# Recurrent attention and a cosine feed-forward on one core: attention matmuls in 64x64 quadrants, half of the cumulative sums, and a new order of steps

## The chip, the cores and the metric

The kernel runs on one core of a Trainium2 chip. A core has a matrix engine (PE, with its weight loads shown as PEld), a vector engine (DVE), a scalar engine that evaluates functions from tables (ACT), a general engine (POOL), a sync engine that here only issues transfers (SP), and 16 DMA engines between HBM and the on-chip memory SBUF. Matmul results land in PSUM, which has eight banks of 128 partitions by 2 KB. The metric is the device time of one execution in microseconds (us); three executions of the kernel before took 195.17, 196.28 and 196.61 us, so the median is 196.28 us.

## The reference, cut to what matters

```python
f = 1.0 / (1.0 + np.exp(-f_logit))                 # (B, H, S, D) = (4, 8, 768, 48)
for t in range(S):
    state = f[:, :, t, :, None] * state + einsum('bhd,bhe->bhde', k[:, :, t], v[:, :, t])
    y[:, :, t] = einsum('bhd,bhde->bhe', q[:, :, t], state)
x = y.transpose(0, 2, 1, 3).reshape(B * S, H * D)  # 3072 tokens x 384
h = x @ w_in                                       # 384 -> 2048
out = (h * np.cos(h)) @ w_out                      # 2048 -> 384
```

Every head holds a 48x48 state that decays row by row with a gate f and takes in one outer product per token. The output of the attention goes token by token through a feed-forward with the activation h*cos(h).

## The kernel before, in words

The recurrence is done in chunks. 256 tokens of one batch make a *pair* of chunks (12 pairs, n = 0..11, three to a batch); partition p holds the tokens 2p (even) and 2p+1 (odd), and the partitions 0..63 and 64..127 are the two chunks g = 0 and 1. For each pair these steps run, named by a prefix and the pair's number; a suffix u = 0, 1 is a half of four heads:

- `f`, `k`, `q`, `v` load the inputs (384 KB each; pairs 0 and 1, the HALVES, load f, k and q in two halves). `ex` and `ln` (lines 321, 324) make sp = ln(1 + exp(-f_logit)), which is -ln f.
- `cum` (lines 335 to 341) forms on PE the running sums of sp for every even and every odd token, and the sum of each chunk: three wide matmuls and four of two columns for each half. `eb` and `ei` (lines 350, 354) take exp of minus and plus the sums.
- `qm`, `km` (line 363) multiply q by the decay and k by its inverse and write bf16. They are transposed, on PE (`tq`, `tk`, then the copy `qkt`) or, for the pairs 4 to 11 (TURN_QK), by a transposing DMA on SP.
- `sc` (line 411) forms the scores, `am` (line 415) masks them on DVE. `ps` (line 434) forms each chunk's outer products, `st` (line 449) adds them to the state, `sz` (line 456) decays it. The state lies in a tile of 128 x (4, 2, 48) in which half of the columns stay zero, and each `sz` is two instructions on 64 partitions, r = 0, 1.
- `y` (line 473) multiplies the masked scores by v, 64 rows and 128 columns of weights at a time; `yi` (line 483) adds q times the state, with 128 rows at a time. Both add into the same two PSUM banks.
- `yb` copies the result, `tx` (line 505) transposes it on PE, `xe` copies it into x.

The feed-forward runs in *units*: units 0 and 1 are 128 tokens each (pair 0), units 2 to 12 are 256 tokens each (pairs 1 to 11). `h` (line 531) is a half of 1024 columns of the first matmul, `co` (line 536) takes the cosine on ACT as a sine, `g` (line 513) multiplies on DVE, `o` (line 547) is a quarter of the second matmul for 128 tokens, `ot` copies, `out` stores. The weights come in eight loads `w` of 768 KB, and `wc` casts them.

The order of all of this is written out by hand: ORDER lists each step with its engine (T is PE, S ACT, V DVE, G POOL, Y SP) and its buffer, and each engine works off its own steps in the order of the list; an engine that waits holds up everything that stands behind it on that engine. `zf` are 24 matmuls on zeros that only keep PE busy. Where ACT goes over from exp/ln to the sine or back, a table load stands between (lines 536 and 586).

Of the kernel before, what the change touches and what calls it, by code (L numbers as in the profile page):

```python
# [9 lines left out]
F32 = mybir.dt.float32  # L10
BF16 = mybir.dt.bfloat16
AF = mybir.ActivationFunctionType
HALF_PI = math.pi / 2.0
# [7 lines left out]
HD = H * D  # L21
NQ = DF // 512
# [12 lines left out]
zf0:T0 zsz.2:V zsp.2:V zqk.2:V zsp.0:V f0.1:S0 zf19:T1 zf21:T0 zf4:T4 zf18:T5 zf15:T4 zf11:T5  # L35
f1.0:S1 f0.0:S zqk.0:V zf8:T4 ex0.1:S ex1.0:S f1.1:Y zf17:T5 k0.1:Y0 ln1.0:S2 cum1.0:T2 eb1.0:S0
ln0.1:S0 cum0.1:T3 ex1.1:S k0.0:Y ex0.0:S ln0.0:S q1.0:Y0 qm1.0:G2 ln1.1:S ei0.1:S0 v0:Y0 tq1.0:T6
km0.1:V0 eb0.1:S1 k1.0:Y1 ei1.0:S1 km1.0:V zf14:T7 zf10:T1 cum0.0:T7 ei0.0:S km0.0:V tk1.0:T
cum1.1:T0 eb1.1:S qkt1.0:V0 q0.1:Y1 qm0.1:G eb0.0:S tk0.1:T1 f2:Y2 tq0.1:T qkt0.1:V1 q0.0:Y ex2:S
ln2:S0 q1.1:Y vb0:G0 ps0.1:T4,5 sc1.0:T2 am1.0:V0 ps0.0:T sc0.1:T6 am0.1:V1 tk0.0:T1 k1.1:Y qm0.0:G  # L40
tq0.0:T cum2.1:T2 sz0.00:V2 qm1.1:G ei1.1:S cum2.0:T qkt0.0:S2 sz0.01:V km1.1:G w0.0:Y0 wc0.0:G
zf6:T6 tq1.1:T7 tk1.1:T qkt1.1:S3 sc0.0:T0 sc1.1:T6 ei2:S2 eb2:S2 st0.1:V0 am0.0:V2 yi0.1:T4 zf12:T5
am1.1:V3 zf16:T0 sz0.10:V2 zsz.3:G v1:Y1 vb1:G1 sz0.11:V y0.0:T5 y0.1:T y1.1:T1,0 yb0.0:S0
ps1.0:T2,3 ps1.1:T y1.0:T yb0.1:V1 tx0.1:T6 w0.1:Y1 zf7:T7 yi1.0:T w0.2:Y2 tx0.0:T7 xe0.1:S0
st1.0:V1 h1.00:T4 sz1.00:V3 yb1.0:S2 zf20:T2 xe0.0:S sz1.01:V yi1.1:T w0.3:Y3 zf1:T1 w1.3:Y4 wc0.1:V
wc0.2:V k2:Y2 yb1.1:S3 zf2:T2 st1.1:V0 sz1.11:V2 wc0.3:V h1.01:T co1.0:S0 q2:Y2 zf13:T2 h0.10:T6
tx1.1:T1 wc1.3:G xe1.1:S1 sz1.10:G g1.0:V0 zqk.1:V km2.1:G0 qm2.1:G h0.01:T2 tx1.0:T0 h0.00:T
xe1.0:S qm2.0:G co0.0:S1 km2.0:G g0.0:V1 h0.11:T co0.1:S2 g0.1:V h1.10:T0 w1.2:Y2 h1.11:T co1.1:S3
h2.31:T4 h2.30:T co2.3:S0 h2.10:T2 h2.11:T h2.21:T6 g1.1:V tq2.1:T0 w1.1:Y3 wc1.1:G g2.3:V4 h2.20:T
co2.1:S1 tq2.0:T1 v2:Y2 g2.1:V wc1.2:V f3:Y0 o3.3:T4 tk2.1:T o1.3:T5 h2.01:T2 h2.00:T co2.2:S2  # L50
tk2.0:T g2.2:V co2.0:S3 qkt2.0:V4 w1.0:Y2 vb2:G2 wc1.0:G o1.2:T qkt2.1:S1 v3:Y0 g2.0:V o0.1:T6
o0.2:T ps2.1:T7 ps2.0:T sc2.0:T0 sc2.1:T2 st2.0:V1 o3.2:T o0.3:T ex3:S o1.1:T k3:Y0 am2.1:V2
am2.0:V1 sz2.01:V3 q3:Y1 f4:Y1 ln3:S2 yi2.0:T7 cum3.1:T2 sz2.00:G cum3.0:T o3.1:T ei3:S0 y2.1:T0
y2.0:T eb3:S1 f5:Y2 o0.0:T km3.1:V2 v4:Y1 km3.0:G qm3.1:G zf22:T1 q5:Y0 yb2.0:V1 vb3:S0 v5:Y2
tx2.0:T7 xe2.0:S2 yi2.1:T ps3.0:T1,2 ps3.1:T q4:Y2 qm3.0:V yb2.1:S0 sz3.00:V2 sz3.01:V tk3.0:T3
tq3.0:T qkt3.0:V2 ot0:S0 tk3.1:T7 out0:Y ex4:S tx2.1:T0 xe2.1:V o1.0:T ln4:S0 tq3.1:T ex5:S h3.11:T0
q6:Y1 ln5:S2 st3.1:V0 qkt3.1:V0 ot1:V1 o3.0:T ot3:V2 sz3.11:V3 sc3.1:T2 sc3.0:T6 k4:Y1 am3.1:V3
h3.10:T co3.1:S0 h3.30:T4 h3.31:T out1:Y am3.0:V0 co3.3:S1 g3.1:V3 h3.20:T2 f6:Y0 y3.0:T6,7 y3.1:T
yb3.0:S3 v6:Y0 yi3.1:T h3.21:T yb3.1:S2 k5:Y2 co3.2:S2 sz3.10:V h3.00:T0 tx3.1:T6 xe3.1:S3 h3.01:T
g3.3:V co3.0:S3 tx3.0:T7 xe3.0:V vb4:G1 g3.2:V cum4.1:T4 cum4.0:T ei4:S1 eb4:S0 h4.31:T6 h4.30:T  # L60
g3.0:V km4.1:G1 km4.0:G qm4.1:G h4.11:T2 h4.10:T o4.3:T0 co4.1:S0 h4.00:T4 g4.1:V2 co4.3:S1 g4.3:V
k6:Y0 o2.3:T1 h4.01:T co4.0:S2 o2.1:T qm4.0:G o4.0:T vb6:V2 o4.2:T vb5:V0 g4.0:V o4.1:T o2.2:T
cum5.1:T2 ot4:S3 cum5.0:T o2.0:T o5.3:T0 ei5:S2 tq4.1:Y3 o5.2:T eb5:S2 sc4.1:T6 ps4.1:T4,5 tq4.0:Y1
sc4.0:T2 ps4.0:T ot2:V0 km5.1:G0 qm5.1:G qm5.0:G am4.1:V2 o5.1:T st4.0:V1 km5.0:G ex6:S ln6:S0
o5.0:T ot5:V1 h4.20:T6 h4.21:T am4.0:V1 sz4.00:G2 f11:Y1 co4.2:S3 g4.2:V f8:Y2 out4:Y tq5.1:Y4
o7.3:T4 cum6.0:T0 yi4.0:T2 sz4.01:G cum6.1:T eb6:S1 o7.1:T y4.1:T3 y4.0:T o7.2:T ei6:S0 yb4.0:V1
yi4.1:T o7.0:T o6.3:T2 yb4.1:S0 st4.1:V0 sz4.10:G3 tx4.1:T5 tq5.0:Y0 ot7:S3 ex8:S sc5.0:T6 ps5.0:T3
ps5.1:T sc5.1:T0 qm6.0:V2 o6.2:T am5.0:V0 f7:Y0 tx4.0:T4 out5:Y am5.1:V3 k7:Y1 ex7:S o6.1:T km6.0:V
sz4.11:G ln7:S2 o6.0:T q8:Y2 xe4.1:S0 km6.1:V xe4.0:S h5.31:T6 h5.30:T h5.11:T0 st5.0:V1 sz5.01:G2
sz5.00:V h5.10:T h5.20:T4 h5.21:T co5.3:S0 g5.3:V1 co5.1:S1 g5.1:V yi5.0:T3 q7:Y0 h5.00:T6 co5.2:S2  # L70
g5.2:V h5.01:T co5.0:S3 k9:Y2 yi5.1:T0 y5.0:T y5.1:T yb5.1:S2 g5.0:V o8.1:T1 yb5.0:S3 o8.3:T
tx5.1:T0 tx5.0:T3 xe5.0:V1 tq6.0:Y2 xe5.1:V out3:Y qm6.1:G tq6.1:Y1 ot6:S1 ln8:S0 ps6.1:T4,5 ps6.0:T
sc6.0:T6 sc6.1:T2 am6.0:V2 sz6.01:V3 o9.0:T0 o9.2:T zsp.1:G h6.10:T6 v7:Y1 h6.11:T am6.1:V1 h6.21:T2
co6.1:S0 sz6.00:V st6.1:V0 sz6.10:G2 h6.20:T co6.2:S1 g6.1:V0 o9.1:T cum7.1:T4 cum7.0:T y6.1:T6,7
out2:Y y6.0:T f10:Y0 ex10:S g6.2:V vb7:V1 o8.2:T eb7:S0 yb6.0:S0 yi6.1:T qm7.0:G1 o9.3:T ei7:S1
o8.0:T h6.00:T2 ot9:V2 tx6.0:T0 yb6.1:V1 sz6.11:G tx6.1:T6 h6.01:T xe6.0:V2 out7:Y ot8:V0 k10:Y0
co6.0:S2 h6.30:T4 h6.31:T xe6.1:V h7.11:T0 g6.0:V h7.20:T6 co6.3:S3 h7.10:T co7.1:S0 h7.21:T km7.0:G
g6.3:V h7.01:T2 co7.2:S1 v8:Y0 vb8:V0 g7.1:V4 f9:Y2 h7.00:T co7.0:S2 km7.1:G h7.31:T4 h7.30:T
co7.3:S3 o10.0:T0 o10.2:T qm7.1:G g7.2:V o10.3:T g7.0:V v9:Y2 tq7.0:Y3 o10.1:T ex9:S sc7.0:T6
ps7.1:T1,2 tq7.1:Y0 out8:Y vb9:G2 ln9:S1 g7.3:V k8:Y1 ps7.0:T sc7.1:T4 o13.3:T3 o13.2:T ln10:S2  # L80
am7.0:V0 cum8.1:T6 cum8.0:T am7.1:V3 y7.1:T4,5 y7.0:T st7.0:V1 ei8:S2 sz7.01:V3 sz7.00:G st7.1:V0
km8.1:V0 o12.0:T1 eb8:S2 qm8.0:V yi7.0:T yb7.0:V2 qm8.1:V yi7.1:T yb7.1:S3 o13.1:T cum9.0:T6
# [575 lines left out]
```

## Time and profile before

| what | value |
|---|---|
| median of three executions | 196.28 us (195.17 to 196.61) |
| span of the profiled execution, first to last instruction | 193.8 us |
| PE busy, share of the span | 179.9 us, 93% |
| DVE busy | 143.4 us, 74% |
| ACT busy (of it 20 table loads of 1.283 us) | 137.3 us, 71% |
| POOL busy | 57.4 us, 30% |
| mean granted PE clock | 0.991 |
| moved by DMA | 34.46 MB, mean 178 GB/s |

The profiled execution's own time is shown as its span, 193.8 us; the median of the executions that were only timed is 2.5 us longer. In a row of groups the first number is the summed busy time and the second the mean duration of one in ns. Matmuls are pipelined, so the duration of one (some 200 to 330 ns) is not what it costs in a stream; that is read from the distance between starts.

### The profile page before, as it was taken

What the parts mean: (1) busy time and instruction counts of PE and PEld (TensorE: products, weight loads), DVE (VectorE), ACT (ScalarE), POOL (GpSimd) and SP (SyncE); (2) the same over time, 40 slices, a digit from 0 to 9 for tenths busy, and PEclk for the clock granted to TensorE, in tenths of its full rate; (3) what the DMA queues carried; (4) which work ended last, traced back from release to release, by engine and by line L of the source; (5) the groups of instructions that cost most, each with busy time, mean ns of one, the idle gap of its engine ahead of it and who ended that gap; (6) DMA issues with size and microseconds to landing.
All of it is one profiled execution on the core that took longest, in us unless ns stands there. A gap on an engine that the chain in (4) does not pass through costs nothing.

```text
span 193.8 us, 5919 instructions
## 1 busy us (share of the span) xinstructions
PE 179.9 (93%) x2560; PEld 132.1 (68%) x2560; DVE 143.4 (74%) x194; ACT 137.3 (71%) x168; POOL 57.4 (30%) x75
## 2 busy tenths in 40 slices
PE   7377979998899999999979999999999999999995
PEld 2255658865678767677758867776776776777762
DVE  5069999994898278579965998589598789868420
ACT  3668668686799988988599896897575494446231
POOL 2249119405410727221017302724510540100000
PEclk9879999999999999999999999999999999999999
DMA  6999999779999899998990850499990024301213
GB/s 145 261 265 346 382 314 309 182 214 263 251 285 282 191 195 174 257 257 160 317 224 5 170 144 3 95 201 189 229 231 3 3 54 98 122 3 41 85 41 122
DMA packets 74106, 34.46 MB, mean 178 GB/s; under 512 B 67424, under 2 KB 72544, under 8 KB 74080
## 3 DMA queue, kind: packets, MB, share of 16 engines
q1 hardware_dynamic: 72496, 33.50, 72.6%
q10 hardware_dynamic: 1584, 0.59, 1.3%
q8 instruction: 20, 0.33, 0.7%
q14 instruction: 6, 0.05, 0.1%
HBM read 25.17 MB, written 4.72 MB: 154 GB/s over the span
## 4 chain that ended last, share of the span: by engine, by line
PE 72%; DVE 11%; ACT 8%; issue 4%; DMA 3%; POOL 1%; ACTq 0%; DVEq 0%; POOLq 0%
PE ps L547 29%; PE ps L531 27%; DVE w_in_bf L190 3%; PE ps L473 3%; DVE am L415 3%; DMA f<-in_f_logit_dram 3%; PE ps L411 2%; PE ps L483 2%; PE ps L335 2%; PE ps L505 2%; ACT f L321 2%; ACT sp L324 1%; DVE st L449 1%; PE ps L434 1%; DVE sz L456 1%
## 5 line engine op out<-in xcount | busy, mean ns | idle before, releaser
L513 DVE TENSOR_TENSOR g<-ps,co 128x1024 bf16<-128x1024 f32 x48 | 61.4, 1307 | 19.2 <-ACT co L536 19.1
L547 PE MATMUL ps<-w_out_bf,g 128*128 128x384 bf16 x384 | 71.4, 326 | 0.0
L531 PE MATMUL ps<-x,w_in_bf 128*128 128x256 bf16 (+1 forms) x624 | 69.3, 264 | 1.5 <-DVE w_in_bf L190 1.4
L536 ACT ACTIVATE co<-ps,halfpi 128x1024 bf16<-128x1024 f32 x48 | 52.5, 1114 | 21.1 <-PE ps L531 20.5
L531 PEld LDWEIGHTS <-w_in_bf 128*128 128x128 bf16 x624 | 56.4, 98 | 11.3 <-DVE w_in_bf L190 2.4
L547 PEld LDWEIGHTS <-g 128*128 128x128 bf16 x384 | 35.0, 98 | 19.7 <-issue 0.2
L415 DVE TENSOR_TENSOR am<-ps,pmask 128x1024 bf16<-128x1024 f32 x24 | 28.6, 1218 | 3.0 <-PE ps L411 2.8
L456 POOL TENSOR_TENSOR sz<-st,b 64x192 bf16<-64x192 f32 x20 | 11.1, 555 | 50.9 <-DVE st L449 49.7
L363 POOL TENSOR_TENSOR qk<-q,b 128x384 bf16<-128x384 f32 x18 | 18.2, 1021 | 15.3 <-DMA q<-in_q_dram 8.7
L363 POOL TENSOR_TENSOR qk<-k,bi 128x384 bf16<-128x384 f32 x15 | 15.4, 1033 | 18.6 <-ACT bi L354 13.3
L536 ACT ACT_TABLE_LOAD x10 | 12.8, 1283 | 4.4 <-PE ps L531 2.0
L363 DVE TENSOR_TENSOR qk<-k,bi 128x384 bf16<-128x384 f32 x9 | 8.1, 912 | 9.4 <-ACT bi L350 6.8
L586 ACT ACT_TABLE_LOAD x10 | 12.8, 1283 | 2.6 <-issue 2.4
L190 ACT COPY x<-ps 128x384 bf16<-128x384 bf16 x13 | 6.0, 478 | 9.2 <-PE ps L505 9.2
L321 ACT ACTIVATE f<-f 128x768 f32<-128x768 f32 (+1 forms) x14 | 10.3, 748 | 2.0 <-DMA f<-in_f_logit_dram 1.9
L335 PE MATMUL ps<-sp,incl 128*128 128x384 bf16 x24 | 8.2, 340 | 3.3 <-ACT sp L324 3.1
L354 ACT ACTIVATE bi<-ps 128x768 f32<-128x768 f32 x10 | 8.1, 812 | 3.7 <-PE ps L341 1.9
L257 PE MATMUL ps<-zero 128*128 128x512 bf16 x24 | 9.3, 493 | 1.4 <-DVE zero L196 1.2
L324 ACT ACTIVATE sp<-f 128x768 bf16<-128x768 f32 (+1 forms) x14 | 10.3, 749 | 0.3
L449 DVE TENSOR_TENSOR st<-ps,sz 128x384 f32<-128x384 f32 x16 | 8.9, 554 | 2.2 <-POOL sz L456 1.4
L411 PE MATMUL ps<-qkt 48*64 48x128 bf16 x384 | 9.2, 220 | 1.0 <-ACT qkt L190 0.8
L473 PE MATMUL ps<-vb,am 64*128 64x48 bf16 x384 | 7.4, 180 | 1.9 <-DVE g L513 1.1
(61 smaller groups left out, 174.9 us busy)
## 6 DMA issues: line engine op xcount, KB each, us to landing
v<-in_v_dram SPq DMA_DIRECT2D x12, 384.0 KB, 5.8
out_dram<-ot SPq DMA_DIRECT2D x24, 192.0 KB, 2.2
f<-in_f_logit_dram SPq DMA_DIRECT2D x10, 384.0 KB, 5.2
k<-in_k_dram SPq DMA_DIRECT2D x10, 384.0 KB, 5.9
q<-in_q_dram SPq DMA_DIRECT2D x10, 384.0 KB, 5.8
g<-in_moe_w_in_dram SPq DMA_DIRECT2D x4, 768.0 KB, 9.7
g<-in_moe_w_out_dram SPq DMA_DIRECT2D x4, 768.0 KB, 5.8
k<-in_k_dram SPq DMA_DIRECT2D x4, 192.0 KB, 5.0
```

The lines of the kernel that those rows point to most:

```text
L321: nc.scalar.activation(out=flat(t.ap), in_=flat(t.ap), func=AF.Exp, scale=-1.0)
L324: nc.scalar.activation(out=s.ap[:, :, :, 0:D], in_=swap(t.ap), func=AF.Ln, bias=1.0)
L363: G.step(f"{nm}{n}.{u}", ("POOL", "DVE"), lambda e, u=u, j=j, src=src, dec=dec: eng(e).tensor_mul(out=qkp[u][j].ap[:, :, :, 0:D], in0=swap ...
L411: nc.tensor.matmul(o[t, r, 2 * a + x, :].rearrange("p (e n) -> p e n", e=2), lhsT=qkv(u)[s, 1, a, g, x, :], rhs=qkv(u)[s, 0, a, g, :, :], ...
L415: G.step(f"am{n}.{u}", ("DVE",), lambda e, u=u, sc=sc: nc.vector.tensor_mul(out=am[u].ap.rearrange("p r b n -> p (r b n)").rearrange("p (y ...
L456: eng(e).tensor_mul(out=new.ap[s, :, r, :].rearrange("p (u a) n -> p u a n", u=2), in0=ap()[s, :, r, :].rearrange("p (u a) n -> p u a n", ...
L473: nc.tensor.matmul(py[g].ap[:, D * i:D * i + D], lhsT=am[u].ap[t, h % 2, h // 2 * 2 + x, :], rhs=vb.ap[t, i, x, :], start=(py[g].first and ...
L513: nc.vector.tensor_mul(out=o.rearrange("p b (n e) -> p b e n", e=2), in0=ph.ap.rearrange("p (b e n) -> p b e n", e=2, n=64), in1=co.ap.rea ...
L531: nc.tensor.matmul(ph.ap[:, i * T:(i + 1) * T].rearrange("p (g t) -> p g t", t=C), lhsT=w_in_bf[:, kk, f0:f0 + 128], rhs=xa[:, :, kk, :], ...
L536: G.step(f"co{m}.{j}", ("ACT",), lambda e, ph=ph, co=co: nc.scalar.activation(out=co.ap, in_=ph.ap, func=AF.Sin, bias=halfpi), reads=[ph], ...
L547: nc.tensor.matmul(po.ap[:, 0:DM], lhsT=gT.ap[:, j, i * C:(i + 1) * C], rhs=w_out_bf[:, j, :], start=(po.first and j == 4 * s), stop=(po.f ...
L586: nc.scalar.preload_act_table_set("natural_log_exp_and_others")
```

## The change

Six things are changed at once.

1. **Cumulative sums.** `cum` forms the sums at odd tokens only: one PSUM bank for a whole pair, two matmuls of 384 columns and eight of two columns (for the cut pairs 0 and 1, two of 192 and four small ones for each half). The sums at an even token differ from those at the odd token behind it by one gate, so q at even tokens is multiplied by 1/f of the odd token and k by f of the odd token. New steps do this: `fx` (ACT, exp(-sp) of the odd tokens), `qa` (DVE, (exp(-f_logit) + 1) * q) and `ka` (POOL or DVE, f * k). `eb` and `ei` are half as wide, and `qm`, `km` read the same factor for even and odd tokens.
2. **Compact states.** The state is a tile of 128 x (4, 48) without zeros; `st` is half as wide, `sz` is one instruction on 128 partitions in place of two on 64, and its buffers need no zeroing.
3. **`y` in quadrants.** Each matmul of `y` is cut into two of 64 output partitions: 768 in place of 384.
4. **`yi` in quadrants.** With the compact state `yi` works on 64 rows and 64 columns: 320 matmuls in place of 136. Each of its two steps writes both banks, one row half for each.
5. **One layout of `qkt`** for both ways of transposing.
6. **A new ORDER** for all steps, with new engines and buffers for many of them.

```diff
+        def lead_q(e, t, w):
+            eng(e).scalar_tensor_tensor(out=w.ap[:, :, 0, :], in0=t.ap[:, :, 1, :], scalar=1.0, in1=w.ap[:, :, 0, :],
+                                        op0=ALU.add, op1=ALU.mult)
+
+        def gate_of(e, t, s):
+            nc.scalar.activation(out=t.ap[:, :, 0, :], in_=s.ap[:, 1, :, 0:D], func=AF.Exp, scale=-1.0)
+
+        def lead_k(e, t, w):
+            eng(e).tensor_mul(out=w.ap[:, :, 0, :], in0=w.ap[:, :, 0, :], in1=t.ap[:, :, 0, :])
...
-            nc.tensor.matmul(o4, lhsT=incl, rhs=w[:, 0:1, :, 0:D].broadcast_to([128, 2, 4, D]),
-                             start=True, stop=False)
-            nc.tensor.matmul(o4[:, 0], lhsT=strict, rhs=w[:, 1, :, 0:D], start=False, stop=False)
-            nc.tensor.matmul(o4[:, 1], lhsT=incl, rhs=w[:, 1, :, 0:D], start=False, stop=False)
...
+            for x in range(2):
+                nc.tensor.matmul(o[:, :, 0:HB], lhsT=incl,
+                                 rhs=w[:, x, :, 0:D].rearrange("p (u h) d -> p u h d", u=un),
+                                 start=(x == 0), stop=False)
...
-            for r in range(2):
-                def decay(e, g=g, r=r, new=new, ap=ap):
-                    s = slice(64 * r, 64 * r + 64)
...
+            def decay(e, g=g, new=new, ap=ap):
+                tot = bt.ap[:, :, HB:].rearrange("p u (a g) -> p u a g", g=2)[:, :, :, g]
...
-                    for g in range(2):
-                        t = slice(64 * g, 64 * g + 64)
-                        i = 4 * u + h
-                        nc.tensor.matmul(py[g].ap[:, D * i:D * i + D], lhsT=am[u].ap[t, h % 2, h // 2 * 2 + x, :],
...
+                    for z in range(2):
+                        for g in (1, 0):
+                            t, w, i = slice(64 * g, 64 * g + 64), slice(64 * z, 64 * z + 64), 4 * u + h
+                            nc.tensor.matmul(py[g].ap[w, D * i:D * i + D],
+                                             lhsT=am[u].ap[t, h % 2, h // 2 * 2 + x, w],
...
+            for a in range(4):
+                for z in range(2):
+                    for r in range(2):
+                        g, h = (r + swap_g) % 2, 2 * a + r
...
+                        nc.tensor.matmul(py[g].ap[w, D * h:D * h + D], lhsT=qkv(a // 2)[t, 0, a % 2, g, z, :],
+                                         rhs=before[g].ap[t, a, :], start=(py[g].first and a == 0),
+                                         stop=(py[g].final and a == 3))
```

How the instructions stand after it: 10 matmuls in a pair's `cum` in place of 14 (12 for the cut pairs), but 568 more in `y` and `yi`; 10 table loads in place of 20; nine input loads issued from ACT's queue in place of three; all four casts of w_in on POOL (before: three on DVE); 14 `fx`, 14 `qa` and 14 `ka` (11 on POOL, 3 on DVE); `sz` 9 on DVE and 11 on POOL (before 20 and 20). The order of PE spends all 24 zero matmuls ahead of the first scores (before: 11 of them), does the sums of the pairs 2 and 3 and all attention of the pairs 0 and 1 but the transposes `tx1` before the first `h`, and then takes the attention of two pairs together, several steps in a row, where the order before spread them singly between `h` and `o`. The first steps of each engine after the change: PE ... sc1.0 tx0.1 tx0.0 cum3 cum2 y1.1 yi1.0 y1.0 h1.01; DVE am0.1 qa1.0 qkt1.1 sz0.0 qm1.0 st0.1 am0.0 st1.0 qkt1.0 am1.1 yb0.1 xe0.1 am1.0 st1.1 xe0.0 yb1.0 xe1.0 xe1.1 qa2 qm2.0 qm2.1 g1.0; POOL km0.1 ka0.0 ka1.1 km0.0 qm0.0 qm1.1 zero ka1.0 km1.0 sz0.1 sz1.0 and the four casts of w_in.

## The prediction

> **What bounds the kernel now.** I read the page first, then the stretches of 10 us, then PE in order of time, then the chain of work that ended last. PE is busy 93% of the span and holds 72% of the chain:
>
> ```profile
> span 193.8 us, 5919 instructions
> ...
> PE 179.9 (93%) x2560; PEld 132.1 (68%) x2560; DVE 143.4 (74%) x194; ACT 137.3 (71%) x168; POOL 57.4 (30%) x75
> ...
> PE 72%; DVE 11%; ACT 8%; issue 4%; DMA 3%; POOL 1%; ACTq 0%; DVEq 0%; POOLq 0%
> ```
>
> The chain says where PE starts to run without gaps. Ahead of this stretch stand DVE's states and its casts of w_in:
>
> ```profile
> 23.94 3.41 DVE w_in_bf L190 x2
> 27.35 0.47 DVE st L449
> 28.02 0.29 issue
> 28.31 1.77 DVE w_in_bf L190
> 30.12 5.46 PE ps L531 x66
> ```
>
> So there are two parts: a head of 30.1 us that other engines set, and PE in a nearly closed stream to its last `o` at 190.3. In the stream a step costs the distance from its start to the next start, not its duration:
>
> ```profile
> 114.09 0.42 PE L411 MATMUL ps<-qkt 48*64 48x128 bf16 x16
> 114.34 0.42 PE L434 MATMUL ps<-vb,qk 64*64 64x48 bf16 x32
> 114.59 0.42 PE L411 MATMUL ps<-qkt 48*64 48x128 bf16 x16
> 114.95 1.47 PE L547 MATMUL ps<-w_out_bf,g 128*128 128x384 bf16 x8
> 116.26 0.33 PE L335 MATMUL ps<-sp,incl 128*128 128x384 bf16 x1
> 116.42 0.25 PE L337 MATMUL ps<-sp,strict 128*128 128x192 bf16 x1
> ...
> 116.59 0.24 PE L341 MATMUL ps<-half,sp 128*128 128x2 bf16 x4
> 116.69 0.32 PE L335 MATMUL ps<-sp,incl 128*128 128x384 bf16 x1
> ...
> 117.19 0.58 PE L473 MATMUL ps<-vb,am 64*128 64x48 bf16 x32
> 117.70 0.82 PE L547 MATMUL ps<-w_out_bf,g 128*128 128x384 bf16 x4
> 118.45 0.53 PE L483 MATMUL ps<-sz,qkt 128*64 128x96 bf16 x16
> 118.92 0.82 PE L547 MATMUL ps<-w_out_bf,g 128*128 128x384 bf16 x4
> ```
>
> Prices from such distances: `h` 0.655 us (0.67 in units 0 and 1), `o` 0.65, `sc` 0.235, `ps` 0.13 for 16 matmuls in quadrants (two steps from 114.34 to 114.59), `cum` 0.43 for a half (116.26 to 116.69). `sc` ahead of `o` takes 0.36 in place of 0.25: when the form of the tiles changes, some 0.095 us are added. Less that, `y` costs 0.21 and `yi` 0.18 (0.17 in the pairs 0 to 3); `tx` 0.167, a transposing step 0.222. From 30.12 to 190.32 these prices sum to 154.9, so PE idles only 5.3 us in 160.2. From the last `o` to the end are 3.5 us.
>
> **The change, PE's work.** In `cum`, 116.26 to 116.42 gives 0.16 for a wide matmul and 116.59 to 116.69 gives 0.027 for a small one: a pair costs 2 x 0.16 + 8 x 0.027 = 0.54, was 0.86: -3.8 over 12 pairs. `y` becomes 32 matmuls in quadrants, a form that `ps` has with the same 48 columns: two times 0.125 = 0.25, was 0.21: +1.0 over 24 steps. Its bounds: 0.20 if the four quadrants pass at twice the rate of the two row tiles in `y` now (-0.2), 0.41 if they pass no faster than those (+4.8); I take `ps`, the same shape. `yi`: before, 14 steps at 0.18 and 6 at 0.17, 3.5; after, 16 of 16 matmuls at 0.125 and 8 of eight at 0.08, 2.6: -0.9. Changes of form in PE's order fall from 69 to 46: -2.2. Together -5.9.
>
> The Trainium skill speaks against cutting `y`: "TensorEngine Tiling (Array Packing)", Instruction Overhead, gives a small matmul a floor of some 60 cycles and warns against splitting a dimension that is already small. By that page, at the page's clock of 2.4 GHz, four quadrants would take 32 x 25 / 4 ns = 0.20 a step, an estimate, and the sum would be 1.2 us lower; the row of `ps` has 0.25, and the sum goes by it.
>
> From the first `h` on, the new order holds: `h` 63.0, `o` 62.4, `cum` of pairs 4 to 11 4.3, transposes 1.8, `sc` 4.7, `ps` 2.4, `y` 5.0, `yi` 2.2, `tx` 3.7, 38 changes of form 3.6: **153.1 us**, with no zero matmul in it.
>
> **The head.** The new order wants all attention of pairs 0 and 1 (but `tx1`) before `h1.01`. Followed by hand: the first gates land at 4.6 as now (both halves of f0 are the first issue of their queues, at 0.73). ACT does `ex` and `ln` at 0.55 each; with half-wide `eb`, `ei`, `fx` (0.3 to 0.5 for 192 columns, between nothing and the 0.49 for 384) it is free at 11.7 and copies `qkt0.1` (1.0); `sc0.1`, then `am0.1` at 13.3. From there DVE is the chain: `am` 4 x 1.2, `qkt` 2 x 0.68, two `st` and one `sz` at 0.35 (192 columns, row of `sz`), `qa1.0` 0.35, `qm1.0` 0.56, `yb` 0.55, `xe` 0.35: 9.0, and 13 gaps of 0.03: 22.7. `y1.0` and `yi1.0` follow; `h1.01` starts at **23.4**. What must not be later: POOL's row of steps from `km0.1` at 8.6 to the first cast of w_in ends at 18 to 19; the landings, one half load each 0.75 us as now and 2.0 for 768 KB, bring w0.1 at 20.2 behind f3 and f2, cast at 21.7. That is 1.7 us of cover; w0.2 and w0.3, cast at 27.0 and 29.0, are wanted at 29.6 and 31. The eleven zeros ahead of `cum1.0` cost 2.4 us at full clock, 4.7 at the half clock of now's first ones (0.43 apart); at 7.4 they end by 9.8 or 12.1, while `ln1.0` is done at 9.9, so up to 2.2 are uncovered.
>
> **The stream.** After 23.4 PE keeps lockstep with `g` through units 0 to 2 (1.31 for two `h`, 1.31 for `g`); `g1.0` starts at 28.3 behind `qa2` and two `qm2`, and o0.0 waits 0.9. Further waits by the same hand count: `sc2.0` for `qkt2.0` on ACT 0.8, `h4.11` for `xe3.0` behind a table load 0.75, smaller ones 0.6: 3.1 until `h6.20` at 83. For the rest I take what the order before loses from 83 on, 3 us, since DVE has 73 us of work there beside PE's 97. Idle together **6.0**.
>
> DVE's new operations are `qa` (128 x 384 from two SBUF operands; the nearest row is L363 on DVE). That row shows a cost of its own:
>
> ```profile
> 10.99 0.56 DVE L363 TENSOR_TENSOR qk<-k,bi 128x384 bf16<-128x384 f32 x1 [6.58 <-ACT bi L350]
> 11.76 2.30 DVE L363 TENSOR_TENSOR qk<-k,bi 128x384 bf16<-128x384 f32 x2 [0.21 <-ACT bi L350]
> ```
>
> Alone it takes 0.56, two beside POOL's multiplies took 1.2 each, and once (154.68) 2.52; the 15 of them average 0.79, an excess of 0.24. On the path lie some 8 in the head and 13 between `h1.01` and `h6.20`, where PE has 56.6 us of steps and DVE 53.5: 21 x 0.24 = 5.0, half of it on the path, **2.5**; bounds 0 and 5. The Trainium skill, "SBUF — State Buffer", section Who interferes with whom, calls this an exclusive lock: a DVE operation with two SBUF inputs waits out a POOL operation that reads SBUF. The 2.52 agrees with it, the eleven of 0.56 or less, seven of them beside POOL work, show that it does not always strike; rival 2 is this mechanism.
>
> Off the path: ACT loses 10 table loads (12.8), 6.5 to 9 of `eb` and `ei`, gains 6.3 of `fx`, 4.2 of `vb` and six issues at 0.5: ACT never ends last for long. POOL gains 9.5 of `ka` and 4.4 of casts, loses `sz`: +7 on 57, covered in the stream by 65% idle time; without that cover `km` and so `tq` come later. SP loses six issues and keeps its transposes. At the end `ot23` takes the buffer that `out19` must free first: 3.7 in place of 3.5.
>
> Sum: 23.4 + 153.1 + 6.0 + 2.5 + 3.7 = 188.7 of span, against 193.8. The median lies 2.5 above the span now: **191.2 us**.
>
> **Rivals.** (1) *The order gives it back*: attention of two pairs in a row makes PE wait for DVE and ACT, idle 12 in place of 8.5: 194.7 to 197. For: DVE at 94% of PE's work until 83. Against: my hand count finds only short waits. (2) *Slower, the blocked DVE operation*: between 24 and 83 us 13 such operations (`qa`, `km`, `qm`, `ka`) block behind POOL, which now has `ka` and all casts there. At e us each beyond what I took, DVE passes PE; slower by 1% from e = 0.55 on (7 us); at 0.7 the time is 200.3. For: 2.52 was seen, POOL is fuller. Against: of the 15 now eleven took 0.56 or less. (3) *The head is no shorter*: w_in lands 3 us later or the zeros run at half clock; closed stream from 27, 194.8. (4) *No blocking*: neither the 2.5 nor the idle beyond 83: 186 to 188. (5) The computation does what it says; the ORDER lists all steps, so that the change does nothing I count as none.
>
> **Chances.** Forecast 0.60 (189 to 194), rival 1 0.13, rival 2 0.13, rival 3 0.08, rival 4 0.06. The range takes in rival 4's upper part, `y`'s and the blocking's bounds and most of rival 1: 187.5 to 197.5. About 1% is what a measurement of this kernel tells from no change (194.3 to 198.2): faster 0.73, within 0.14, slower 0.13.
>
> **What would show it.** L-rows of `cum` 6.8 us of starts in place of 10.6; `y` 0.25 a step; first `h` near 23.4 and closed from there; PE idle after it under 9; table loads 10. Wrong it is if the first `h` comes after 27, if DVE's `qa`, `km` and `qm` average over 1.0, or if PE stands before `sc`, `y` or `tx` for DVE for more than 8 us in all.

## The result, and the profile after

The change makes the kernel slower: **213.37 us** (median, 212.59 to 214.74) against 195.85 us (195.17 to 196.61) for the kernel before on the same chip, a ratio of 1.088 with a 95% interval of 1.082 to 1.094. The prediction was 191.2 us with a range to 197.5, so even its slower rivals stop short of this.

The page of the kernel after, in the lines that answer to those shown of before, and two that the prediction did not show: the granted clock of PE in 40 slices and the queue that brings instructions.

```profile
span 211.8 us, 6990 instructions
...
PE 185.9 (88%) x3084; PEld 137.4 (65%) x3084; DVE 138.2 (65%) x197; ACT 124.6 (59%) x172; POOL 66.0 (31%) x76
...
PEclk9995558999976999969999799999999999999999
...
q8 instruction: 24, 0.39, 0.8%
...
PE 53%; DMA 9%; issue 9%; POOL 4%; ACT 3%; DVE 2%; SPq 1%; POOLq 0%
```

PE's share of the chain falls from 72% to 53%, and "issue", time in which an engine waited for nothing that the profile shows, goes from 4% to 9%. PE's clock, granted in full or at half, is at half from 16.5 to 33.6 us and in three later stretches (60.9 to 67.7, 91.6 to 95.0, 118.9 to 122.4). The same two lines of the page of before:

```profile
PEclk9879999999999999999999999999999999999999
...
q8 instruction: 20, 0.33, 0.7%
```

The chain of work that ended last, after the change, shows where the issue time lies:

```profile
52.86 3.36 PE ps L569 x20
57.74 0.76 PE ps L569 x4
58.80 2.68 issue
...
87.81 3.89 issue
...
116.46 2.79 issue
...
196.12 12.36 PE ps L569 x76
```

And the timeline of PE around the first of these (start, duration, line, operation, count; in brackets the idle time before it and what ended it). PE stops in the middle of one step `y`: 5 of its 32 matmuls had gone since 58.4, beside `yi`; the other 27, and the next `y`, follow 2.68 us later. Their operands had been there for the first 5.

```profile
57.67 0.83 PE L569 MATMUL ps<-w_out_bf,g 128*128 128x384 bf16 x4
...
58.49 0.21 PE L490 MATMUL ps<-vb,am 64*64 64x48 bf16 x2
...
58.58 0.22 PE L490 MATMUL ps<-vb,am 64*64 64x48 bf16 x3
61.48 1.00 PE L490 MATMUL ps<-vb,am 64*64 64x48 bf16 x59 [2.68 <-issue]
```

The list of PE's waits (line that waited, what it waited for, us in total, times, longest) says the same: the two largest have no other engine and no transfer of data behind them. In the kernel before no wait of PE for "issue" reaches 0.2 us.

```profile
PE ps L490 <- issue: 9.3, 4, 3.9
PE ps L452 <- issue: 2.8, 1, 2.8
PE ps L553 <- DVE g L535: 1.7, 1, 1.7
```

The reading that follows from the q8 line: PE's instructions come in transfers of 16,384 bytes, 20 before and 24 after, for 5,120 and 6,168 loads and matmuls. That is 256 instructions a transfer, or **128 pairs of weight load and matmul**. The count follows PE's pairs in the kernels below, too: 19 transfers for 2,516 pairs, 21 for 2,700, 23 for 2,944. In the records of the transfers and matmuls, numbering the matmuls of the program from 0, the stops stand at 223, 351, 863, 1247, 1374, 1885 and 2397: at 95 + 128j, give or take two. And each ends 1.3 to 1.6 us after such a transfer has ended. At the six stops up to 1885 the transfer of the piece started 1.7 to 4.0 us after PE had crossed into the piece before it and took 1.0 to 1.2 us, so that PE, beside the input loads, got 128 pairs in 4.2 to 6.5 us. The stop at 2397 is the exception: its transfer began 0.1 us ahead of the crossing, and the 128 pairs took 2.1 us. By the prices of the prediction the shortest 128 pairs in a row need some 2.5 us before the change and 1.0 us after it; stretches under 2 us are 0 before and over 200 after.

The Trainium skill, "Runtime: NRT & Kernel Launch", section Instruction fetch mechanics, describes such a stream in blocks of 16 KiB and calls the cost of a block's boundary "mostly hidden". The blocks agree with the records (16,384 bytes, 256 instructions); the cost does not: here it is up to 3.9 us a boundary.

### The profile page after: what moved, and what is told of

The parts are those of the page before. It is cut to its first block, busy times and chain, and to the rows that moved or that the text cites. A ratio compares the mean times of both kernels' runs of the same rounds, so it can differ in the third digit from the quotient of the medians.

```text
span 211.8 us, 6990 instructions
## 1 busy us (share of the span) xinstructions
PE 185.9 (88%) x3084; PEld 137.4 (65%) x3084; DVE 138.2 (65%) x197; ACT 124.6 (59%) x172; POOL 66.0 (31%) x76
## 4 chain that ended last, share of the span: by engine, by line
PE 53%; DMA 9%; issue 9%; POOL 4%; ACT 3%; DVE 2%; SPq 1%; POOLq 0%
PE ps L569 22%; PE ps L553 21%; DMA qkt<-qk 5%; DMA f<-in_f_logit_dram 4%; POOL qk L382 3%; PE ps L490 2%; PE ps L527 2%; PE ps L429 1%; PE ps L505 1%; SPq L398 1%; PE ps L452 1%; PE ps L352 1%; PE ps L409 1%; ACT co L558 1%; DVE g L535 1%
## 5 line engine op out<-in xcount | busy, mean ns | idle before, releaser
L382 POOL TENSOR_TENSOR qk<-k,bi 128x384 bf16<-128x384 f32 x17 | 18.1, 1070 | 16.9 <-DVE k L336 8.7
L490 PE MATMUL ps<-vb,am 64*64 64x48 bf16 x768 | 11.3, 198 | 9.4 <-issue 9.3
L191 ACT CAST yb<-ps 128x384 bf16<-128x384 f32 x15 | 6.8, 479 | 19.3 <-PE ps L505 13.4
L336 POOL TENSOR_TENSOR k<-k,f 128x384 f32<-128x384 f32 (+1 forms) x11 | 10.1, 924 | 24.9 <-ACT f L333 24.7
L490 PEld LDWEIGHTS <-am 64*64 64x64 bf16 x768 | 9.3, 118 | 11.3 <-issue 11.0
L191 DVE COPY x<-ps 128x384 bf16<-128x384 bf16 x18 | 6.3, 355 | 14.9 <-PE ps L527 11.1
L191 DVE COPY ot<-ps 128x384 f32<-128x384 f32 x13 | 7.2, 552 | 10.1 <-PE ps L569 9.9
L191 ACT COPY ot<-ps 128x384 f32<-128x384 f32 x11 | 5.2, 475 | 12.6 <-PE ps L569 9.8
L191 DVE CAST yb<-ps 128x384 bf16<-128x384 f32 x9 | 5.0, 556 | 10.3 <-PE ps L505 6.7
L329 DVE SCALAR_TENSOR_TENSOR q<-f,q 128x384 f32<-128x384 f32 (+1 forms) x14 | 7.5, 550 | 4.4 <-DMA q<-in_q_dram 4.3
```

Source lines behind the costliest of these rows:

```text
L191: (nc.scalar.copy if e == "ACT" else eng(e).tensor_copy)(out=o, in_=i)
L336: eng(e).tensor_mul(out=w.ap[:, :, 0, :], in0=w.ap[:, :, 0, :], in1=t.ap[:, :, 0, :])
L382: G.step(f"{nm}{n}.{u}", ("POOL", "DVE"), lambda e, u=u, j=j, src=src, dec=dec: eng(e).tensor_mul(out=qkp[u][j].ap[:, :, :, 0:D], in0=swap ...
L490: nc.tensor.matmul(py[g].ap[w, D * i:D * i + D], lhsT=am[u].ap[t, h % 2, h // 2 * 2 + x, w], rhs=vb.ap[t, i, x, :], start=(py[g].first and ...
```

## The experiments

Three theories were put against each other first. **T1**: the time goes to PE's supply of instructions, which steps made of small quadrants outrun. **T2**: matmuls in 64x64 quadrants are themselves slow, or slow the steps that hold them. **T3**: the time goes to waits for other engines and loads that the hand count missed.

### The same steps, other boundaries

The first nine matmuls on zeros, 512 columns each, are cut into eight of 64 columns. That puts 63 more pairs ahead of all that follows, and the boundaries of the pieces fall elsewhere.

```diff
-            G.step(f"zf{i}", ("PE",), lambda e, dump=dump: nc.tensor.matmul(
-                dump.ap, lhsT=zero[:, 0:128], rhs=zero, start=True, stop=True), writes=[dump])
+            def zeros(e, dump=dump, cut=8 if i < 9 else 1):
+                for c in range(cut):
+                    s = slice(512 // cut * c, 512 // cut * c + 512 // cut)
+                    nc.tensor.matmul(dump.ap[:, s], lhsT=zero[:, 0:128], rhs=zero[:, s], start=True, stop=True)
```

> The changed kernel, in which the first nine zero matmuls of 512 columns are each cut into eight of 64 columns: the same columns in the same head, 63 more load and matmul pairs ahead of everything. Nothing is left out. Theory 1 (supply of the program): PE's program comes in pieces of 256 instructions (128 pairs), and PE stops where it has used up a piece sooner than the next one is there. All stops then come 63 or 64 matmuls of the work earlier or 64 later: not in y0.1, y1.1, y3.1, y5.1 and ps9.1 but near yi1.1, h1.01, yi2.1, y5.0, ps6.1 and yi7.0. Their sum by pieces used in under 4.5 us is 14.8 in place of 20.0 us, so the time is 3 to 7 us shorter, 206 to 211. Theory 2 (the quadrant matmuls stop PE themselves, by banks or by the form): the stops stay in y0.1, y1.1, y3.1, y5.1, ps9.1 and the time within 1% of 213.4. Theory 3 (waits on transfers or engines that the profile doesn't name): as theory 2.

Measured: 212.3 us (two runs, 213.84 and 210.75). The stops are at the matmuls 479, 863, 991, 1374, 1501 and 1885 of the longer program, again 95 + 128j, and so in other steps: `h`, `ps`, `yi`, `y`, `ps`, `yi`. The `h` is a step that has no quadrants at all. A seventh wait, 2.14 us at 351 between `yi` and `sc`, ends 1.3 us after such a transfer too, but the profile puts it down to DVE's copy `yb`; which of the two it was is open. The timeline of PE in this kernel, where the stop of 3.89 us stood before: it is now 63 matmuls earlier in the work, and PE passes the old place without one.

```profile
88.81 0.24 PE L493 MATMUL ps<-vb,am 64*64 64x48 bf16 x7
91.35 0.40 PE L493 MATMUL ps<-vb,am 64*64 64x48 bf16 x25 [2.30 <-issue]
91.57 0.31 PE L508 MATMUL ps<-sz,qkt 64*64 64x48 bf16 x16
```

T2 and T3 fall as the cause of these stops: neither has a reason to move with the count of instructions. The time does not part them: it lies in the range of T2 and T3, and T1's (206 to 211) was missed. By the prices the boundaries meet fewer short stretches here, yet PE's waits for "issue" are 11.8 us against 12.4. So T1 told where the stops are and not how long.

### `y` in rows, all else as after

The loop of `inner` is that of before (64 rows by 128 columns, 384 matmuls); compact states, `yi` and `ps` in quadrants, sums and order are those of after.

```diff
-                    for z in range(2):
-                        for g in (1, 0):
-                            t, w, i = slice(64 * g, 64 * g + 64), slice(64 * z, 64 * z + 64), 4 * u + h
+                    for g in range(2):
+                        t = slice(64 * g, 64 * g + 64)
+                        i = 4 * u + h
```

> The changed kernel with y back in 64 rows by 128 columns (384 matmuls in place of 768), all else and the order as changed. Theory 1: 768 PE instructions less; pieces used in under 4.5 us lose 5.8 us in place of 20.0, so stops of 14.6 us fall to about 4 and the half clock that follows them to under 15 us: 197 to 202. Theory 2: the stops in y go, the 3.0 in ps9.1 stays, as ps is unchanged: 200 to 204. Theory 3: no change but -1.0 for y and +3 for changes of form: 213 to 216.

Measured: 204.25 us, a ratio of 1.039 (1.026 to 1.053). In this order the quadrants of `y` cost **9.1 us**, though a step's price differs by 0.04 us, 1.0 us in all. The time is 2.25 us above T1's range and 0.25 above T2's, so it does not part the two. The list of waits does:

```profile
PE ps L452 <- issue: 4.4, 2, 2.5
PE ps L490 <- issue: 2.0, 1, 2.0
```

Two stops stay in `ps` (2.5 and 1.9 us), where `yi` and `ps` still stand together in quadrants. The third is at matmul 223, as in the kernel after, and in `y` (L490), which has no quadrants any more; by T2 it had to go.

### `y` in quadrants, all else as before

The reverse: the kernel before, its order too, with only the loop of `inner` from after.

```diff
-                    for g in range(2):
-                        t = slice(64 * g, 64 * g + 64)
+                    for z in range(2):
+                        for g in (1, 0):
+                            t, w, i = slice(64 * g, 64 * g + 64), slice(64 * z, 64 * z + 64), 4 * u + h
```

> The kernel before with y alone cut into quadrants (768 in place of 384 matmuls), old order, old sums, old states. Price of the matmuls: +1.0 us, less 1 to 2 for fewer changes of form. Theory 1: its attention stands spread between h and o, so few pieces are used in under 4.5 us: stops of 2 to 6 us, most of them at the start and near ps9.0: 196 to 203. Theory 2: stops of 1 to 4 us inside y as in the changed kernel, five or more of them: 206 or more. Theory 3: 195 to 197.

Measured: 201.85 us, 1.027 (1.016 to 1.038), 5.0 us over the kernel before on the same chip. There is one stop for instructions, and it is the longest of all, at matmul 351. Its place on the timeline of PE in this kernel is between a transposing step and a matmul on zeros that has no operand to wait for; behind it comes the first `h`:

```profile
23.56 0.34 PE L506 MATMUL ps<-ident,yb 128*128 128x128 bf16 x3 [0.22 <-DVE yb L190]
28.58 0.59 PE L257 MATMUL ps<-zero 128*128 128x512 bf16 x1 [4.69 <-issue]
...
29.60 0.63 PE L532 MATMUL ps<-x,w_in_bf 128*128 128x128 bf16 x4
```

The kernel before has its first `h` as matmul 295, at 23.46 us. Here it is matmul 359, beyond the boundary at 351, and comes at 29.60. Only 64 more pairs ahead of it cost 6.1 us. After the change it is matmul 410, at 29.26.

### Fewer loads beside the work

The kernel after, but a load into an input buffer that was filled once brings one head of eight (48 KB in place of 384): most of the later inputs are left out of the computation.

```diff
+            at = (val.whole.pool.name, val.whole.slot)
+            n = 1 if at in filled and h1 - h0 == H else h1 - h0
...
-            in_=tok.rearrange("h (p e) d -> p h (e d)", e=2)), writes=[val])
+            eng(e).dma_start(out=val.ap.rearrange("p h e d -> p h (e d)")[:, 0:n],
+                             in_=tok.rearrange("h (p e) d -> p h (e d)", e=2)[:, 0:n])
```

> The changed kernel, in which every load of q, k, v and f_logit into a buffer that has been filled once brings one head of eight (48 KB in place of 384), so that most of the later inputs are left out of the computation; all instructions of PE are the same. Theory 1: the pieces of the program no longer stand behind loads: their transfer begins under 1 us after it is asked for, as in the stretches without loads, and is there 2.6 to 3.7 us after. Stops after 45 us fall from 11.4 to under 4 us, at the same places or gone; the head's two stops stay, since its loads stay: 197 to 203. Theory 2: the stops stay as long as they are: 211 to 213. Theory 3 (waits for loads): the time falls by what was waited for loads, some 5 us: 207 to 209.

Measured: 199.54 us, 1.015 (1.003 to 1.027). The instructions are the same; PE's waits for "issue" fall from 12.4 to 4.8 us, and beyond 32 us there is no half clock. The waits for data stay (10.0 us after, 9.7 here).

```profile
PE ps L495 <- issue: 2.9, 3, 1.3
PE ps L457 <- issue: 1.9, 1, 1.9
```

So it is the loads that make a piece late. At the stops 863, 1374 and 1885 the transfer starts 0.1, 1.5 and 0.8 us after the crossing, where it was 2.0, 3.9 and 2.0 us, and takes 0.9 to 1.0 us in place of 1.2. Where it is held up beside the loads is not shown.

### Only the halved sums

The kernel before in its own order with the halved sums, `fx`, `qa` and `ka`, and the old states and forms of `y`, `yi` and `ps`; it has one buffer more for `f`.

```diff
+            G.step(f"fx{n}{u}", ("ACT",), lambda e, t=t, s=s: gate_of(e, t, s), reads=[s], writes=[t], table="E")
+            G.step(f"qa{n}{u}", ("DVE",), lambda e, t=t, w=wq: lead_q(e, t, w), reads=[t], writes=[wq])
+            G.step(f"ka{n}{u}", ("POOL", "DVE"), lambda e, t=t, w=wk: lead_k(e, t, w), reads=[t], writes=[wk])
...
-cum2.1:T2 ... cum2.0:T ... km2.1:G0 qm2.1:G
+cum2:T2 ... ka2:G km2.1:G0 qa2:V qm2.1:G
```

> The kernel before in its own order of steps, with only the first part of the change: cumulative sums at the odd tokens, the two lead steps for q and k, half-wide eb and ei; old states, old rows for y, yi and ps. 2516 pairs of weight load and matmul against 2560, so the shortest stretch of 128 pairs is 2.53 us by the prices, as before. T1 (the time after the change was lost to TensorE's supply of instructions, which 64x64 quadrants outrun): no stop over 1.5 us at a matmul 95+128j after the first h, TensorE's work 3.8 us less, 191 to 194 us. Rival (the sums cost more than they save: fx on ScalarE 0.53 us and qa 0.59 us on VectorE a tile stand in the path): 196 to 200 us.

Measured: **213.3 us**, 1.085 (1.078 to 1.093), and both theories had it wrong. The supply is not at fault here (0.4 us of waits for "issue"). PE waits for data, by the list of its waits:

```profile
PE ps L524 <- DVE yb L193: 6.7, 3, 3.3
PE ps L410 <- POOL qk L382: 6.4, 4, 2.7
```

The second line is the head, where `ka` and the products stand in one queue; the first `h` comes at 32.2 us, and half clock takes 27 us of the head. The first line is DVE holding PE up, as in rival 2 of the prediction, but not by blocked operations: `ka` waits for the load of k, and the copy `yb`, on which PE waits for 3.3 us, stands behind it and two more. The timeline of DVE shows it.

```profile
56.13 0.56 DVE L336 TENSOR_TENSOR k<-k,f 128x384 f32<-128x384 f32 x1 [2.04 <-DMA k<-in_k_dram]
56.80 0.56 DVE L382 TENSOR_TENSOR qk<-k,bi 128x384 bf16<-128x384 f32 x1
57.52 1.10 DVE L329 SCALAR_TENSOR_TENSOR q<-f,q 128x384 f32<-128x384 f32 x1 [0.17 <-DMA q<-in_q_dram]
58.55 0.55 DVE L193 CAST yb<-ps 128x384 bf16<-128x384 f32 x1
```

Half clock of 6.8 us follows this wait, and as much a second one like it.

### Halved sums for tiles 2 to 11, and off DVE

Tiles 0 and 1 have the old sums, so the head is the old one; `ka`, `qm` and `km` of the others are all on POOL.

```diff
+            if cut:
+                continue
             G.step(f"fx{n}{u}", ("ACT",), lambda e, t=t, s=s: gate_of(e, t, s), reads=[s], writes=[t], table="E")
...
-ka3:V km3.1:V2
+ka3:G km3.1:G2
```

> The kernel before in its own order, with halved sums for tiles 2 to 11 only (tiles 0 and 1, and so the head, as before), the lead step of k and the products qm and km of these tiles all on POOL, so that VectorE's copies of y stand behind nothing but qa. If the halved sums alone had lost x_sums its time by the waits they bring (head 8.8 us, VectorE's copy of y behind k's lead step 6.7 us and the half clock behind it), this one has first h at 23.5 us as before and TensorE's work 3.2 us less: 191.5 to 195 us. If fx on ScalarE and qa on VectorE cost it in the steady part, 196 to 200 us.

Measured: 203.16 us, 1.036 (1.029 to 1.042), above both ranges. The head is 0.9 us late only (first `h` at 24.36), but PE's waits for data are 18.0 us against 11.3 before, the longest again for `yb` behind DVE's row (3.3 us). The halved sums alone, laid into an order made for other steps, cost more than the 3.2 us of PE that they save. It is not the supply: no wait for "issue" reaches 0.2 us. Which of `fx`, `qa` and `ka` costs most was not taken apart.

### The new order and the halved sums, without new quadrants

The order of after; `y`, `yi` and the states as before, so each `sz` is two instructions again.

```diff
-sz1.0:G2 yb0.1:V0 yi1.1:T7,3
+sz1.00:G2 sz1.01:G yb0.1:V0 yi1.1:T3
```

> The order of steps of the kernel after, with the halved sums, but no quadrants where there were none: y in 64x128 rows, yi in its old form, states in their wide layout with two sz steps each. 2516 pairs; by the prices the shortest 128 pairs take 2.27 us, 100 stretches under 3.5 us against 882 after. T1 (supply): stops under 3 us in all, full clock but for the first 10 us or so, TensorE's work 3.0 us over that of the prediction: 192 to 197 us. Rival (the new order itself loses the time, by waits at its in-order heads): 203 to 212 us.

Measured: 202.62 us, 1.033 (1.026 to 1.039). Above T1's range, just below its rival's. PE's waits for "issue" are down to 1.9 us, but the first `h` comes at 27.81 us (23.46 before), and from there to the end of the last `o` PE takes 169.9 us (167.0 before), though its work on PE is 2.9 us less by the prices. The order and the sums cost 6.2 us, the quadrants and compact states the other 10.8. Within these, `y` has 9.1; the compact states and `yi` hold the 1.6 left, which the intervals do not tell from nothing.

### The supply by itself

Behind the last matmul of the kernel before stands a tail that nothing waits for: 768 matmuls on zeros in quadrants, then 384 of 128 x 128 by 128 columns. No input load runs any more.

```diff
+    def tail(d, quads):
+        for i in range(768 if quads else 384):
+            g, z = i % 2, i // 2 % 2
+            t, w = (slice(64 * g, 64 * g + 64), slice(64 * z, 64 * z + 64)) if quads else (slice(0, 128),) * 2
+            nc.tensor.matmul(d[g if quads else 0].ap[w, 0:48 if quads else 128], lhsT=zero[t, w],
+                             rhs=zero[t, 0:48 if quads else 128], start=True, stop=True)
```

> The kernel before with a tail behind its last matmul, which nothing waits for: 768 matmuls in 64x64 quadrants on zeros (48 columns, as in y, in two banks in turn), then 384 matmuls of 128x128 by 128 columns. T1 (supply by pieces of 256 instructions, asked for one piece ahead): the quadrants run 128 pairs in 1.0 us and then stop until the next piece is there, 2.5 to 5 us a piece, stops at matmuls 95+128j of the program, 15 to 30 us for 768; the wide ones, 60 ns or more a pair, run without a stop. T2 (quadrants are slow of themselves when they follow each other for long): 768 of them at an even pace, no stops at these places. T3 (the stops were waits of this kernel's other engines): 768 in about 6.1 us (7.9 ns each).

Measured, on the timeline of PE in the tail:

```profile
192.55 2.00 PE L265 MATMUL ps<-zero 64*64 64x48 bf16 x221
196.75 1.23 PE L265 MATMUL ps<-zero 64*64 64x48 bf16 x128 [2.20 <-issue]
200.48 1.91 PE L265 MATMUL ps<-zero 64*64 64x48 bf16 x128 [2.50 <-issue]
204.21 1.91 PE L265 MATMUL ps<-zero 64*64 64x48 bf16 x128 [1.82 <-issue]
207.94 1.91 PE L265 MATMUL ps<-zero 64*64 64x48 bf16 x128 [1.82 <-issue]
211.39 2.82 PE L265 MATMUL ps<-zero 64*64 64x48 bf16 x54 [1.54 <-issue]
```

This is what T1 expected. (The last row has the last 35 quadrants and the first wide matmuls.) The quadrants run in bursts of 128, some 8.3 ns each at full clock (the first 128 in 1.05 us), and a burst comes every 3.45 to 3.73 us: 1.1 from its first matmul until the next transfer starts, some 1.2 for the transfer, 1.3 to 1.5 until PE goes on. All 768 take some 19 us. The wide ones behind them, 56 ns each at full clock, run without a stop. So this is the supply with no loads beside it: 3.5 to 3.7 us for 128 pairs. From 198.0 on the clock is at half for 17 us, though no single stop passes 2.5 us.

### More zeros in the head

In the kernel after half clock begins at 16.5 us, ahead of the first stop. Eight more matmuls on zeros fill three waits of PE there. The same was done to the new order without new quadrants.

```diff
-ZEROS = 24
+ZEROS = 32
...
-tk0.0:T2 tk1.1:T3 sc0.1:T4
+tk0.0:T2 zf24:T6 zf25:T6 zf26:T6 tk1.1:T3 sc0.1:T4 zf27:T7 zf28:T7 zf29:T7
...
-ps0.1:T
+ps0.1:T zf30:T6 zf31:T6
```

> The kernel after with eight more zero matmuls (128x512) in three waits of TensorE in the head: three behind tk0.0, three behind sc0.1, two behind ps0.1. In the kernel after the half clock of 16.6 to 33.6 us begins ahead of the first stop for instructions (19.8 us), and the kernel with the new order and no quadrants has it too (14.5 to 28.2). H1 (it comes from TensorE's waits of 0.6 to 0.8 us at 13 to 16.6 us, where all zeros are used up): full clock till after 20 us, first h at 26.5 to 28.3 us instead of 29.3, 210 to 212.5 us. H2 (it comes from the 64x64 quadrants or the stops for instructions): half clock from 14 to 17 us as before, first h 29.3 to 30, 213 to 215 us.

> The kernel in the new order with halved sums and no quadrants for y, yi and ps, with the same eight zero matmuls more in the head. H1: full clock through the head, first h at 24.5 to 26.5 us instead of 27.8, 199 to 201.5 us. H2: half clock from 14.5 us as without them, first h 27.8 to 28.5, 202 to 204 us.

Measured: 212.87 us for the first. The second took 201.58 us in the profiled execution and 204.4 to 205.0 in three others, on both sides of the 202.62 without the zeros, so it does not settle whether that kernel gained. On the clock H1 holds in both: half clock begins at 21.6 us, as the stop for instructions ends, and at 23.4 us in the second. The columns here are the window, the busy time of PE, PEld, DVE, ACT and POOL, PE's granted clock, the DMA share and GB/s; first the kernel after, then the one with more zeros:

```profile
14.00:17.00 3.00, 1.73 (x70) 1.36 (x72) 2.53 (x5) 2.09 (x4) 2.79 (x4) 0.92 1.29 264
17.00:20.00 3.00, 2.99 (x102) 2.40 (x92) 2.60 (x5) 2.16 (x3) 0.79 (x2) 0.50 1.06 374
```

```profile
14.00:17.00 3.00, 2.50 (x72) 1.41 (x76) 2.98 (x5) 1.36 (x2) 2.72 (x4) 1.00 1.29 262
17.00:20.00 3.00, 1.83 (x82) 1.32 (x75) 2.60 (x5) 1.97 (x3) 1.02 (x2) 1.00 1.08 367
```

On the time it missed: the first `h` stays where it was (29.26 and 29.38 us; in the second kernel 27.30 in place of 27.81). PE came to matmul 223 0.9 us sooner and stopped 0.9 us longer, for the piece ended its transfer at 20.41 (20.55 after): PE goes on at 21.88 us here and at 21.86 after. In the head of this kernel the supply sets the pace, and a faster PE only waits for it.

### The same instructions, spread

The kernel after with steps `o` later in PE's order, so that the short stretches get wide matmuls between them. Nothing else is changed; of the lines of ORDER only PE's steps are shown. (Counted against the other steps of PE it is 20 steps that stand later, not 26.)

```diff
-o4.2:T2 o5.2:T3 o5.0:T o4.0:T sc4.0:T6 sc5.0:T0 sc4.1:T4 o5.3:T o4.1:T cum6:T6 o4.3:T ps5.1:T4
+o4.2:T2 sc4.0:T6 sc5.0:T0 o4.0:T o5.0:T3 sc4.1:T4 o4.1:T cum6:T6 o4.3:T ps5.1:T4
-ps5.0:T y4.0:T5,7 y4.1:T yi4.0:T sc5.1:T0
+ps5.0:T y4.0:T5,7 y4.1:T yi4.0:T o5.2:T
```

> The kernel after, with the same instructions; only 26 of the 64 steps o0.0 to o15.3 stand later in TensorE's order, between the steps of the attention that follows (largest moves: o5.2 by 13 places, o5.3 by 11, o6.2 and o1.3 by 9). By the prices the short stretches of 128 pairs grow: the one from matmul 735 from 1.84 to 4.47 us, from 863 3.23 to 4.20, from 1247 2.38 to 4.19, from 1759 1.03 to 3.46; the two in the head (95 and 223) stay. Changes of form cost 2.1 us more. T1 (supply of instructions): the stops at 863 (2.87), 1374 (4.08) and 1885 (2.98) shrink to under 0.5, some 2 and under 1 us, the half clock behind at least two of them goes, those at 223 and 351 stay: 203 to 207 us. Rival (the time lies elsewhere, or the moved steps leave waits for data where they stood): 210 to 214 us.

Measured: **215.08 us**, 1.098 (1.090 to 1.106). On the stops T1 is right: those at 863 and 1885 are gone, the one at 1374 is 1.91 us in place of 4.08 (from start to start of the two matmuls). On the time the rival is right. PE's waits for "issue" fall from 12.4 to 5.4 us, and those for data rise from 10.0 to 16.2:

```profile
PE ps L491 <- issue: 4.6, 3, 2.0
PE ps L410 <- POOL qk L383: 2.3, 2, 1.5
PE ps L430 <- DVE g L536: 2.1, 2, 1.2
PE ps L554 <- DVE g L536: 1.8, 1, 1.8
PE ps L491 <- DVE am L434: 1.4, 1, 1.4
```

An `o` that is moved behind a scores step no longer covers the wait ahead of it. So part of what PE loses at a stop the other engines use to catch up, and a stop taken away at the cost of cover gives nothing back. Nor does the half clock behind 33 us shrink, as T1 expected: it is 13.65 us again, but two of its three stretches, from 51.8 and from 109.8 us, now stand behind waits for data of 0.6 to 1.1 us.

## Why the prediction was wrong

PE's waits of 0.2 us and more, summed from the list of waits of each kernel, the first `h`, and the time, side by side:

| kernel | waits for "issue", us | waits for data, us | first `h`, us | time, us |
|---|---|---|---|---|
| before | 0 | 11.3 | 23.46 | 195.9 |
| after | 12.4 | 10.0 | 29.26 | 213.4 |
| after, `y` in rows | 6.4 | 12.2 | 28.05 | 204.3 |
| after, fewer loads | 4.8 | 9.7 | 27.91 | 199.5 |
| after, spread | 5.4 | 16.2 | 29.27 | 215.1 |
| new order and sums, old forms | 1.9 | 13.9 | 27.81 | 202.6 |
| before with halved sums | 0.4 | 22.3 | 32.21 | 213.3 |

**The step that failed is the sum of idle time: "Idle together 6.0", and with it the head of 23.4.** Both count what PE waits for from other engines. That PE itself could run out of instructions was in no term, in no rival, and in none of the unknown costs. Nor was half clock behind the head in any. The change adds 524 pairs and puts them close together. The stops that follow take 13.8 us, measured from start to start (12.4 by the list, which leaves out the short ones), and half clock, much of it right behind them, some 7.7. Not all of the loss is there: the order and the sums without the quadrants are 6.2 us slower than the kernel before, with 1.9 us of such waits.

Point by point, against the span of 188.7 that was forecast and the 211.8 measured:

- **PE's prices were right.** By starts `cum` takes 0.53 us, `y` 0.26 to 0.27, `yi` 0.127 for 16 matmuls, `ps` 0.126, a change of form 0.09 to 0.10. They bear out the 153.1 from the first `h` on. The price taken from `ps` held. By the Trainium skill, "TensorEngine Tiling (Array Packing)", Instruction Overhead, `y` would have been 0.20, an estimate that the runs show a little too low; its clock of 2.4 GHz is not on that page.
- **The head: 29.26 in place of 23.4.** Of the 5.9 us, 3.2 are the stops at 223 and 351. The other 2.7 are the hand count's own, and without `y`'s quadrants, too, the first `h` comes at 27.3 to 28.1: it followed DVE, but `am0.1` starts at 14.47 instead of 13.3, and PE's `tq1.1` waits 0.65 us for POOL's `qm1.1`, which ends at 15.02. A right hand count would not have saved the forecast, though: matmul 351 goes at 28.33 to 28.35 us in after, after with zeros and after spread, whatever PE did ahead of it, and the first `h` is matmul 410. Rival 3 had this size, for other reasons.
- **From the first `h` to the last `o`: 26 us over the prices.** The stops at 95 + 128j take 10.7 (2.87, 0.27, 4.08, 2.98, 0.46). Half clock, 18.0 us of it, takes about 7.7, worked out from the steps that it lengthens; 13.65 us of it stand in windows right behind the three long stops. What is left is 7.6, of which 5.2 are waits for data behind the first `h`; it stands against the 6.0 and 2.5 of the prediction, which together were about right.
- **The blocked DVE operation** (rival 2) came, but seldom: DVE's `qm` means 0.97 us, `km` 0.74, `qa` 0.55, and PE's waits for DVE before `sc`, `y` and `tx` are 1.5 us in all. Where it struck hardest, two `qm2` took 3.36 us beside two casts on POOL, and PE's longest wait for data, 1.7 us for the `g` behind them, follows (first DVE, then POOL):

```profile
34.20 3.36 DVE L382 TENSOR_TENSOR qk<-q,b 128x384 bf16<-128x384 f32 x2
37.48 5.10 DVE L535 TENSOR_TENSOR g<-ps,co 128x1024 bf16<-128x1024 f32 x4
```

```profile
33.62 3.53 POOL L191 CAST w_out_bf<-g 128x1536 bf16<-128x1536 f32 x2
```

- ACT, POOL and the ten table loads came as forecast; the tail is as long as before, without the 0.2 us that the prediction added.
- **Rival 1** (the order gives it back) was partly true, and its price was too low: the order and the sums without new quadrants take 202.6 us, not 194.7 to 197. In this kernel 4.4 us lie in the head, and PE's waits for data grow by 2.6.

Of the signs named for a wrong forecast the first came (first `h` after 27), the other two did not. Three things stay open. The parts do not add up cleanly: `y`'s quadrants cost 9.1 us in the new order and 5.0 in the old one. The 6.2 us of the order and the sums were not taken apart. And an order was not found in which the halved sums pay; one made anew for them might.

The Trainium skill, "TensorE: Matmul & The Clock Gate", Part 1: The HAM clock gate, tells of free-running windows of some 3.4 us, and of half clock behind a window that was idle. The records agree with the windows (lengths here are 3.41, 6.83, 10.24, 17.07 us), but the tail of the experiment and the head after the change went to half clock without a whole idle window, under waits of at most 2.5 and 0.8 us.

## What to carry to other kernels

Count instructions as a resource of PE: work out how long each 128 pairs of load and matmul in a row take by their prices, and hold that against the supply, here 3.5 to 3.7 us with no loads beside it and 4.2 to 6.5 us at most stops beside heavy loads. Cutting matmuls into quadrants at the same price per step can still cost much, most of all ahead of the first wide matmuls, where loads are thickest and each piece of the program sets the pace. And an order fitted by hand to its steps is hard to change in part: the halved sums and `y`'s quadrants, each put alone into the old order, and the new order without the new quadrants all came out slower. Last, taking stops away is not the same as taking time away: a stop can cover a wait for data.

## What was not expected of the hardware

- PE's program arrives 256 instructions at a time, and not far ahead: at the stops the transfer of a piece began 1.1 us after PE had crossed into the piece before it with no loads, and up to 4.1 us after it beside loads; PE went on 1.3 to 1.6 us after its end. Where PE did not stop, the transfer began anywhere from 1.5 us ahead of the crossing to 3.9 us behind it (in the kernel after).
- The stops carry no name in the profile but "issue". What shows them is that PE halts inside a step, at a multiple of 128 pairs from the last halt, give or take two.
- In the head of several kernels with different work PE goes on at the same instant (21.86, 21.88, 21.87, 21.89 us in after, after with zeros, after spread, new order): what PE does does not set it. With `y` in rows it is 22.13 us and in the new order with zeros 21.61. That the load traffic sets it fits, but was not tested in the head alone.
- Quadrants pass at 8.3 ns a pair at full clock and 13.3 at half; the loaded head is supplied with one pair in 48 ns (128 in 6.2 us).
